# Moving squares between two phases of an attention and MLP kernel, splitting masks, and reordering value matmuls

## The chip, the cores and the metric

One core of a Trainium2 chip runs the whole program. The metric is the device time of one execution in microseconds (us). Several executions are timed; a kernel that is compared with the kernel before runs in alternating rounds with it on the same chip. Ratios are computed as the mean time of one kernel's fast runs over that of the other's of the same rounds, so they are not quite the ratio of the medians that are quoted.

## The reference, cut to what matters

```python
# q, k, v: 8 batches, 8 heads, 576 positions, head size 64; s: 8 x 8 x 576
scores = scale * q @ k.T + minimum(-(cum_i - cum_j), 0)     # causal, cum = cumsum(relu(s))
attn   = softmax(scores); x = attn @ v                       # 4608 tokens x 512
out    = gelu(x @ w_in) @ w_out                              # 512 -> 2048 -> 512
```

## The kernel before, the parts that matter

The MLP runs over nine chunks of 512 tokens. In chunk c it does the first layer (`l1_item`, eight items of eight matmuls, each with a gelu on ScalarE), then the second layer (`l2_item`, 16 groups). Beside the second layer stands the attention of the next batch b = c + 1: scores, exponentials, masks, value matmuls. Between the exponentials and the gelus the kernel loads ScalarE's table of functions anew, 16 times in all: `exp_set` and `gelu_set` are the loads, 1.28 us each in the trace.

```python
def square_v(b, st):                       # only the sum is used; sq is written and never read
    sq = work.tile([128, S * 2], bf16, tag="sq", bufs=1, name="sq")
    nc.scalar.activation(sq[:n_st, : H * D], raws[b, "v"][...], func=AF.Square,
                         accum_out=sumv[:n_st, b, st : st + 1])

def l1_item(c, f2, n0=0, n1=NB):
    h_ps = ps.tile([128, 2, NB], fp32, tag="sc", bufs=2, name="h_ps")     # ... cut
    ...                                     # 8 matmuls into h_ps
    nc.scalar.activation(gT_of[c][:, f2*2 : f2*2+2, n0:n1], h_ps, func=AF.Gelu)

# second layer of chunk c, side work of batch b = c + 1 (chunks 1 to 6):
sc_at = (2, 5, 7, 9) if b < 4 else (2, 5, 8, 11)     # groups at which scores stand
...
for st in range(ST):
    side[sc_at[3]].append((square_v, b, st))          # after the last exponentials
side[sc_at[3]].append((gelu_set,))                    # then the table for the next first layer
```

The squares feed a check that the fast formula is safe; they are needed at the end only.

Of the kernel before, what the change touches and what calls it, by code (L numbers as in the profile page):

```python
# [19 lines left out]
def kernel(  # L20
# [21 lines left out]
    ST = 5  # L42
# [151 lines left out]

    def square_qk(g, i):

        sq = work.tile([128, S * 2], bf16, tag="sq", bufs=1, name="sq")
        nc.scalar.activation(
            sq, raws[0, "qk"][:, i, g, :], func=AF.Square, scale=D ** -0.5,
            accum_out=ssq[:, g, i : i + 1],  # L200
        )

# [5 lines left out]

    def square_v(b, st):
        n_st = 128 if st < ST - 1 else SL  # L210
        sq = work.tile([128, S * 2], bf16, tag="sq", bufs=1, name="sq")
        nc.scalar.activation(  # L212
            sq[:n_st, : H * D], raws[b, "v"][:n_st, st].rearrange("p h d -> p (h d)"), func=AF.Square,
            accum_out=sumv[:n_st, b, st : st + 1],
        )

# [142 lines left out]
                P[:, 2 * h2 : 2 * h2 + 2, o : o + 512], s_ps[h2], func=AF.Exp, scale=scale  # L359
            )  # L360

    def mk_item(b, g, u):
        P = P_of[b, g]
        o = UO[u]
        d = P[:, :, o : o + 512].rearrange("p e (g c) -> p e g c", c=256)[:, :, :, 0:128]
        nc.vector.tensor_tensor(  # L366
            d, d, tri_bf.unsqueeze(1).unsqueeze(1).to_broadcast([128, 4, 2, 128]), op=MULT
        )
        if u == 1:
            d = P[:, :, o + 448 : o + 512]  # L370
            nc.vector.tensor_tensor(
                d, d, tri_bf[:, :64].unsqueeze(1).to_broadcast([128, 4, 64]), op=MULT
            )
# [40 lines left out]
    def filler(n, lhsT=None):  # L414

        f_ps = yps.tile([128, NB], fp32, tag="mlp", bufs=2, name="f_ps")
        for _ in range(n):
            nc.tensor.matmul(  # L418
                f_ps, lhsT=zero[:, :128] if lhsT is None else lhsT, rhs=zero, start=True, stop=True
            )  # L420
# [7 lines left out]
    def av_item(b, g, it, later=False):  # L428
        P = P_of[b, g]
        n = 128 if it < ST - 1 else SL  # L430
        o_ps = ps.tile([128, 4, D + 1], fp32, tag="av", bufs=2, name="av")
        for h in range(4):
            for i, (jt, off) in enumerate(BLK[it]):
                nc.tensor.matmul(  # L434
                    o_ps[:, h, :],
                    lhsT=P[:, h, off : off + 128],
                    rhs=vv[b % 2][:, jt, 4 * g + h, :],
                    start=(i == 0), stop=(i == len(BLK[it]) - 1),
                )
        if g == 0:  # L440
            x_of[b, it] = work.tile([128, H * D], bf16, tag="x", bufs=6, name="x")
        rc = work.tile([128, 4], fp32, tag="rc", bufs=3, name="rc")
        nc.vector.reciprocal(rc[:n], o_ps[:n, :, D])  # L443
        nc.vector.tensor_tensor(  # L444
            x_of[b, it][:n, g * 256 : g * 256 + 256].rearrange("p (h d) -> p h d", d=D),
            o_ps[:n, :, 0:D],
            rc[:n].unsqueeze(2).to_broadcast([n, 4, D]),
            op=MULT,
        )
        if g == HG - 1 and b > 0 and not later:  # L450
            to_xT(b, it)
# [92 lines left out]
    sc_first(1, 0, (1,))  # L544
    av_item(0, 0, 0)
    filler(1)
    av_item(0, 0, 1)
    sc_first(0, 1, (1,))
    mk_item(0, 1, 0)
    sc_first(1, 1, (0,))  # L550
    av_item(0, 1, 0)
    av_item(0, 1, 1)
    sc_first(1, 1, (1,), 0)
    to_xT(0, 0, True)
    filler(2)
    to_xT(0, 1, True)
    filler(2)
    mk_item(0, 0, 1)
    scale_v(0, 2)
    mk_item(0, 1, 1)  # L560
# [9 lines left out]
    for c in range(NCH):  # L570
        b = c + 1
        if c > 0 and b + 1 < B:
            load_qks(b + 1)
            load_v(b + 1, nc.gpsimd)
        if c == 0:

            late = [
                [], [], [], [(av, 0, 0, 2), (av, 0, 1, 2)], [(av, 0, 0, 3)],
                [(av, 0, 1, 3), (to_xT, 0, 2, True)], [(to_xT, 0, 3, True)],
                [(scale_v, 0, 4), (av, 0, 0, 4)],  # L580
                [(av, 0, 1, 4), (to_xT, 0, 4, True)],
            ] + [[]] * 7
            for half in range(2):
                for f2 in range(FT // 2):
                    l1_item(0, f2, half * 256, half * 256 + 256)
                    for f, *a in late[8 * half + f2]:
                        f(*a)
                    if f2 % 2 and 3 <= 8 * half + f2 <= 11:
                        square_v(0, 4 * half + f2 // 2 - 1)
        else:  # L590
            for f2 in range(FT // 2):
                l1_item(c, f2)
                for g, it in late_of.get(c, [])[f2 : f2 + 1]:
                    av(c, g, it)
                if b < B and f2 < HG:
                    tr_qk(b, 0, f2)
                    tr_qk(b, 1, f2)
                if b < B and f2 == 2:
                    den_col(b)
                    for st in range(2):  # L600
                        scale_v(b, st)
                if b < B and f2 == 3:
                    for st in range(2, ST):
                        scale_v(b, st)
                if b < B and 4 <= f2 < 4 + HG:
                    absmax(b, f2 - 4)
                if c == 2 and f2 == 7:
                    cert_decay()
                if c == 1 and 1 <= f2 <= ST:
                    square_v(c, f2 - 1)  # L610
        if b < B:
            if c == 0:
                for g in range(HG):
                    for i in range(2):
                        tr_qk(b, i, g)
                den_col(b)
            exp_set()
            if c == 0:
                load_qks(2)
                load_v(2, nc.gpsimd)  # L620
                side = [[] for _ in range(16)]
                side[0] = [(sc, b, 0, 0), (scale_v, b, 0), (scale_v, b, 1), (mk, b, 0, 0)]
                side[3] = [(sc, b, 1, 0), (mk, b, 1, 0)]
                side[5] = [(sc, b, 0, 1), (av, b, 0, 0), (av, b, 0, 1)]
                side[6] = [(scale_v, b, 2), (av, b, 1, 0, True), (mk, b, 0, 1)]
                side[7] = [(sc, b, 1, 1), (av, b, 1, 1, True), (to_xT, b, 0, True)]
                side[8] = [(scale_v, b, 3), (av, b, 0, 2), (to_xT, b, 1, True), (gelu_set,), (mk, b, 1, 1)]
                side[9] = [(av, b, 0, 3)]
                side[11] = [(av, b, 1, 2, True), (scale_v, b, 4), (square_qk, 0, 0), (square_qk, 0, 1)]
                side[12] = [(av, b, 1, 3, True), (square_qk, 1, 0), (square_qk, 1, 1)]  # L630
                side[13] = [(to_xT, b, 2, True)]
                side[14] = [(to_xT, b, 3, True)]
                groups(c, (0, 1), side[:8])
                for sub in (2, 3):
                    groups(c, (sub,), side[4 * sub : 4 * sub + 4])
            else:

                side = [[] for _ in range(16)]
                sc_at = (2, 5, 7, 9) if b < 4 else (2, 5, 8, 11)
                for at, (g, u) in zip(sc_at, [(0, 0), (1, 0), (0, 1), (1, 1)]):  # L640
                    side[at].append((sc, b, g, u))
                for st in range(ST):
                    side[sc_at[3]].append((square_v, b, st))
                side[sc_at[3]].append((gelu_set,))
                for at, (g, u) in zip((5, 8, 10 if b < 4 else 11, 12 if b < 4 else 14), [(0, 0), (1, 0), (0, 1), (1, 1)]):
                    side[at].append((mk, b, g, u))
                for at, (g, it) in zip((6, 7, 9, 10), [(0, 0), (0, 1), (1, 0), (1, 1)]):
                    side[at].append((av, b, g, it))
                if b < 4:
                    side[12].append((av, b, 0, 2))  # L650
                    side[13].append((av, b, 1, 2, True))
                    side[14].append((to_xT, b, 2, True))
                if c == 1:
                    side[0].extend([(absmax, c, 0), (absmax, c, 1)])
                    side[3].append((cert_exp,))
                for sub in range(4):
                    groups(c, (sub,), side[4 * sub : 4 * sub + 4])
        else:
            for sub in range(4):
                l2_item(c, (sub,), store=(c, sub) < LAST)  # L660
                if c == B - 1:
                    (cert_1, cert_2, cert_3, cert_4)[sub]()
# [172 lines left out]
```

## Time and profile before

| | before |
|---|---|
| median of three runs | 318.3 us (318.27 to 318.76) |
| span of the profiled run | 316.6 us, granted clock 1.000 |
| TensorE / ScalarE / VectorE busy | 96% / 61% / 63% |
| chunk 0's first layer, its second layer, chunk 1's first layer begin | 18.93, 36.22, 56.60 us |
| from chunk 1's first layer to the last second layer (the "body") | 241.11 us |

Below, PE is TensorE, ACT ScalarE, DVE VectorE. A line of a timeline gives start, length, engine, source line, operation, output<-input, shapes, count, and in brackets the idle time before with what ended it. A line of the table of waits gives waiter, what was waited for, total us, number and longest. Shown ends of matmuls are modelled: one of the second layer is shown with 379 ns and the next starts after 216, so a true wait is about 0.16 us longer than the shown one.

### The profile page before, as it was taken

Reading aid. Unit: us, or ns where it says so; the run is one execution under the profiler, and the core shown is the slowest. Engines: PE = TensorE matmul, PEld = TensorE weight load, DVE = VectorE, ACT = ScalarE, POOL = GpSimd, SP = SyncE. Lnnn points to the kernel's source line nnn. Section 1 sums busy time; section 2 is a strip of 40 time slices with the busy share of each in tenths; the row PEclk is TensorE's granted clock in tenths of the full one; section 3 lists DMA queues with packets and bytes.
Section 4 is the critical chain, followed back from the end, with each engine's and each line's share of the span. In section 5 each row is a group of like instructions: output and inputs, shape, how many; then the busy total and the mean of one; then the engine's idle time right before and its main releaser. Section 6 shows DMA issues by size and latency. Waiting matters only on the chain. (4 is left out here: it accounts for less than half of the span.)

```text
span 316.6 us, 6078 instructions
## 1 busy us (share of the span) xinstructions
PE 303.5 (96%) x2480; PEld 156.1 (49%) x2523; DVE 199.9 (63%) x400; ACT 192.9 (61%) x256; POOL 52.9 (17%) x72
## 2 busy tenths in 40 slices
PE   8999998999999999999999999999999999999993
PEld 3587754444554455445444444444444545444441
DVE  7876658699769766965697559945894632250020
ACT  2786976887765687564956676657756685105500
POOL 8543440125070006000240004000000000000000
PEclk9999999999999999999999999999999999999999
DMA  7999999669869215932399158412110321010012
GB/s 133 220 230 209 226 212 277 129 111 211 187 176 185 64 53 155 196 59 76 97 176 162 66 101 160 35 56 79 52 24 34 101 51 25 33 69 33 1 69 75
DMA packets 30980, 36.48 MB, mean 115 GB/s; under 512 B 15648, under 2 KB 20000, under 8 KB 30944
## 3 DMA queue, kind: packets, MB, share of 16 engines
q0 software_dynamic: 11552, 23.07, 38.5%
q1 hardware_dynamic: 19248, 12.80, 15.7%
q8 instruction: 22, 0.36, 0.5%
q14 instruction: 14, 0.11, 0.2%
q10 hardware_dynamic: 144, 0.13, 0.1%
HBM read 36.85 MB, written 9.44 MB: 146 GB/s over the span
## 5 line engine op out<-in xcount | busy, mean ns | idle before, releaser
L466 PE MATMUL h_ps<-xT,w_in_r 128*128 128x512 bf16 (+1 forms) x626 | 131.7, 357 | 2.8 <-ACT gT L471 2.0
L482 PE MATMUL o_ps<-w_out_r,gT 128*128 128x512 bf16 x549 | 132.3, 379 | 2.2 <-issue 1.3
L471 ACT ACTIVATE gT<-h_ps 128x1024 bf16<-128x1024 f32 (+1 forms) x80 | 74.6, 938 | 63.7 <-PE h_ps L466 62.9
L466 PEld LDWEIGHTS <-w_in_r 128*128 128x128 bf16 x640 | 60.0, 98 | 56.5 <-issue 2.9
L482 PEld LDWEIGHTS <-gT 128*128 128x128 bf16 x576 | 52.0, 98 | 56.5 <-issue 3.1
L358 ACT ACTIVATE P<-sc_ps 128x1024 bf16<-128x1024 f32 x56 | 54.3, 1021 | 30.7 <-PE sc_ps L343 30.7
L122 POOL DMA_DIRECT2D raw_v<-in_v_dram x40 | 34.0, 864 | 119.7 <-ACT sq L212 107.4
L492 DVE COPY o_sb<-o_ps 128x512 f32<-128x512 f32 x32 | 22.1, 691 | 48.5 <-PE o_ps L482 48.5
L443 DVE RECIPROCAL rc<-av 128x4 f32<-128x4 f32 (+1 forms) x80 | 14.0, 175 | 40.2 <-PE av L434 40.2
L187 DVE STREAM_TRANSPOSE qkT<-raw_qk 128x576 f32<-128x576 f32 x32 | 37.4, 1242 | 0.9 <-DMA raw_qk<-in_k_dram 0.6
L434 PEld LDWEIGHTS <-P 128*128 128x128 bf16 x576 | 27.2, 98 | 17.4 <-DVE x L444 1.6
L444 DVE TENSOR_TENSOR x<-av,rc 128x256 bf16<-128x256 f32 (+1 forms) x80 | 33.8, 423 | 3.0
L204 DVE TENSOR_REDUCE amx<-raw_qk 128x2 f32<-128x2304 bf16 x14 | 35.1, 2535 | 0.0
L434 PE MATMUL av<-vv,P 128*128 128x65 bf16 x576 | 30.4, 193 | 1.0 <-DVE x L444 0.7
L220 DVE TENSOR_TENSOR vv<-raw_v,wb 128x512 bf16<-128x512 f32 (+1 forms) x40 | 26.0, 689 | 3.2 <-DMA raw_v<-in_v_dram 3.2
L366 DVE TENSOR_TENSOR P<-P,tri_bf 128x1024 bf16<-128x1024 bf16 x32 | 21.9, 684 | 8.8 <-ACT P L358 8.8
L212 ACT ACTIVATE sq<-raw_v 128x512 bf16<-128x512 f32 (+1 forms) x40 | 25.1, 628 | 0.8
L343 PE MATMUL sc_ps<-qkT 32*128 32x256 bf16 (+2 forms) x560 | 18.2, 250 | 0.1
L343 PEld LDWEIGHTS <-qkT 32*128 32x128 bf16 x560 | 11.7, 92 | 12.7 <-issue 12.0
L418 PE MATMUL f_ps<-zero 128*128 128x512 bf16 x32 | 11.2, 468 | 1.3 <-DVE zero L150 1.2
L497 ACT ACT_TABLE_LOAD x8 | 10.3, 1283 | 0.9 <-PEq L819 0.7
L500 ACT ACT_TABLE_LOAD x8 | 10.3, 1283 | 0.1
(79 smaller groups left out, 90.2 us busy)
## 6 DMA issues: line engine op xcount, KB each, us to landing
out_dram<-o_sb SPq DMA_DIRECT2D x35, 256.0 KB, 2.2
raw_v<-in_v_dram POOLq DMA_DIRECT2D x32, 256.0 KB, 6.3
raw_qk<-in_q_dram POOLq DMA_DIRECT2D x7, 576.0 KB, 9.0
raw_qk<-in_k_dram POOLq DMA_DIRECT2D x7, 576.0 KB, 11.9
w_in_r<-in_moe_w_in_dram POOLq DMA_DIRECT2D x4, 512.0 KB, 12.0
w_out_r<-in_moe_w_out_dram POOLq DMA_DIRECT2D x4, 512.0 KB, 16.4
raw_v<-in_v_dram POOLq DMA_DIRECT2D x8, 128.0 KB, 8.0
raw_qk<-in_q_dram POOLq DMA_DIRECT2D x2, 288.0 KB, 5.6
```

The costliest lines, as they stand in the source:

```text
L122: eng.dma_start(out=t[:n_st, st, :, :], in_=bass.AP(tensor=v.tensor, offset=v.offset + b * H * S * D + st * 128 * D, ap=[[D, n_st], [S * D ...
L187: nc.vector.transpose(qkT[b % 2][:, i, g, :S, :].rearrange("p s e -> p (s e)").bitcast(fp32) .rearrange("p (l j) -> p j l", j=LT), raws[b, ...
L204: nc.vector.tensor_reduce(amx[:, b * HG + g], raws[b, "qk"][:, :, g, :], axis=AX, op=ALU.max, apply_absolute_value=True,)
L212: nc.scalar.activation(sq[:n_st, : H * D], raws[b, "v"][:n_st, st].rearrange("p h d -> p (h d)"), func=AF.Square, accum_out=sumv[:n_st, b, ...
L220: nc.vector.tensor_tensor(vv[b % 2][:n_st, st, :, 0:D], raws[b, "v"][:n_st, st, :, :], w.unsqueeze(2).to_broadcast([n_st, H, D]), op=MULT,)
L343: nc.tensor.matmul(s_ps[h // 2][:, h % 2, off : off + n], lhsT=qk[r, 1, g, jt * 128 : jt * 128 + 128, e], rhs=qk[r, 0, g, i0 : i0 + n, e], ...
L358: nc.scalar.activation(P[:, 2 * h2 : 2 * h2 + 2, o : o + 512], s_ps[h2], func=AF.Exp, scale=scale)
L434: nc.tensor.matmul(o_ps[:, h, :], lhsT=P[:, h, off : off + 128], rhs=vv[b % 2][:, jt, 4 * g + h, :], start=(i == 0), stop=(i == len(BLK[it ...
L444: nc.vector.tensor_tensor(x_of[b, it][:n, g * 256 : g * 256 + 256].rearrange("p (h d) -> p h d", d=D), o_ps[:n, :, 0:D], rc[:n].unsqueeze( ...
L466: nc.tensor.matmul(h_ps[:, i, :], lhsT=w_in_r[:, ko, ft * 128 : (ft + 1) * 128], rhs=xT[:, ko, c * NB + n0 : c * NB + n1], start=(ko == 0) ...
L471: nc.scalar.activation(gT_of[c][:, f2 * 2 : f2 * 2 + 2, n0:n1], h_ps, func=AF.Gelu)
L482: nc.tensor.matmul(y_of[c, sub], lhsT=gT[:, ft, sub * 128 : (sub + 1) * 128], rhs=w_out_r[:, ft, :], start=(ft == 0), stop=(ft == FT - 1),)
```

## The change

The intent: take the squares of v away from the stretch between the last exponentials and the next gelus, and tighten the start of the kernel and chunk 0's second layer. Cut to its core:

```diff
 def square_qk(g, i):                         # batch 0
-    sq = work.tile([128, S * 2], bf16, tag="sq", bufs=1, name="sq")
-    nc.scalar.activation(sq, raws[0, "qk"][:, i, g, :], ...)
+    r = raws[0, "qk"][:, i, g, :]
+    nc.scalar.activation(r, r, ...)
 def square_v(b, st):
-    sq = work.tile([128, S * 2], bf16, tag="sq", bufs=1, name="sq")
+    sq = work.tile([128, H * D], bf16, tag="sq", bufs=2, name="sq")
 ... mk_item takes h0, h1: a part of the heads
 # start
+    mk_item(0, 1, 0, 0, 2)
     av_item(0, 0, 1)
+    mk_item(0, 1, 0, 2, 4)
     sc_first(0, 1, (1,))
-    mk_item(0, 1, 0)
-    sc_first(1, 1, (0,))
+    filler(1)
     av_item(0, 1, 0)
     av_item(0, 1, 1)
+    sc_first(1, 1, (0,), 0)
+    to_xT(0, 0, True)
+    filler(1)
+    to_xT(0, 1, True)
     sc_first(1, 1, (1,), 0)
-    to_xT(0, 0, True)
-    filler(2)
-    to_xT(0, 1, True)
-    filler(2)
 # first layer, chunks 1 to 7
-                if c == 1 and 1 <= f2 <= ST:
-                    square_v(c, f2 - 1)
+                if f2 < ST and c < B:
+                    square_v(c, f2)
 # chunk 0's second layer
-                side[6] = [(scale_v, b, 2), (av, b, 1, 0, True), (mk, b, 0, 1)]
-                side[7] = [(sc, b, 1, 1), (av, b, 1, 1, True), (to_xT, b, 0, True)]
-                side[8] = [(scale_v, b, 3), (av, b, 0, 2), (to_xT, b, 1, True), ...]
+                side[6] = [(av, b, 1, 0, True), (av, b, 1, 1, True), (scale_v, b, 2), (mk, b, 0, 1)]
+                side[7] = [(to_xT, b, 0, True), (sc, b, 1, 1)]
+                side[8] = [(to_xT, b, 1, True), (scale_v, b, 3), (av, b, 0, 2), ...]
 # later second layers
-                for st in range(ST):
-                    side[sc_at[3]].append((square_v, b, st))
                 side[sc_at[3]].append((gelu_set,))
```

More of the change, by code (lines that the diff above doesn't have):

```diff
@@ L195, in square_qk @@
     def square_qk(g, i):
-        sq = work.tile([128, S * 2], bf16, tag="sq", bufs=1, name="sq")
+        r = raws[0, "qk"][:, i, g, :]
         nc.scalar.activation(
-            sq, raws[0, "qk"][:, i, g, :], func=AF.Square, scale=D ** -0.5,
+            r, r, func=AF.Square, scale=D ** -0.5,
             accum_out=ssq[:, g, i : i + 1],
@@ L210, in square_v @@
         n_st = 128 if st < ST - 1 else SL
-        sq = work.tile([128, S * 2], bf16, tag="sq", bufs=1, name="sq")
+        sq = work.tile([128, H * D], bf16, tag="sq", bufs=2, name="sq")
         nc.scalar.activation(
-            sq[:n_st, : H * D], raws[b, "v"][:n_st, st].rearrange("p h d -> p (h d)"), func=AF.Square,
+            sq[:n_st], raws[b, "v"][:n_st, st].rearrange("p h d -> p (h d)"), func=AF.Square,
             accum_out=sumv[:n_st, b, st : st + 1],
@@ L360, in sc_item, with mk_item @@
             )
-    def mk_item(b, g, u):
+    def mk_item(b, g, u, h0=0, h1=4):
         P = P_of[b, g]
         o = UO[u]
-        d = P[:, :, o : o + 512].rearrange("p e (g c) -> p e g c", c=256)[:, :, :, 0:128]
+        d = P[:, h0:h1, o : o + 512].rearrange("p e (g c) -> p e g c", c=256)[:, :, :, 0:128]
         nc.vector.tensor_tensor(
-            d, d, tri_bf.unsqueeze(1).unsqueeze(1).to_broadcast([128, 4, 2, 128]), op=MULT
+            d, d, tri_bf.unsqueeze(1).unsqueeze(1).to_broadcast([128, h1 - h0, 2, 128]), op=MULT
         )
@@ L624 @@
                 side[5] = [(sc, b, 0, 1), (av, b, 0, 0), (av, b, 0, 1)]
-                side[6] = [(scale_v, b, 2), (av, b, 1, 0, True), (mk, b, 0, 1)]
-                side[7] = [(sc, b, 1, 1), (av, b, 1, 1, True), (to_xT, b, 0, True)]
-                side[8] = [(scale_v, b, 3), (av, b, 0, 2), (to_xT, b, 1, True), (gelu_set,), (mk, b, 1, 1)]
+                side[6] = [(av, b, 1, 0, True), (av, b, 1, 1, True), (scale_v, b, 2), (mk, b, 0, 1)]
+                side[7] = [(to_xT, b, 0, True), (sc, b, 1, 1)]
+                side[8] = [(to_xT, b, 1, True), (scale_v, b, 3), (av, b, 0, 2), (gelu_set,), (mk, b, 1, 1)]
                 side[9] = [(av, b, 0, 3)]
```

## The prediction

> **What bounds the kernel now.** I began with the page's table of busy time and its groups of instructions (columns: line, engine, operation, output<-inputs, count | busy us, mean ns of one | idle us before, by releaser).
>
> ```profile
> PE 303.5 (96%) x2480; PEld 156.1 (49%) x2523; DVE 199.9 (63%) x400; ACT 192.9 (61%) x256; POOL 52.9 (17%) x72
> ...
> L466 PE MATMUL h_ps<-xT,w_in_r 128*128 128x512 bf16 (+1 forms) x626 | 131.7, 357 | 2.8 <-ACT gT L471 2.0
> L482 PE MATMUL o_ps<-w_out_r,gT 128*128 128x512 bf16 x549 | 132.3, 379 | 2.2 <-issue 1.3
> ```
>
> TensorE (PE) is the bound and is nearly full, so only its gaps can be won. Part of the idle time is not real: L482 should have 576 records and shows 549, and a missing one of 0.22 us leaves a gap put down to "issue" (8 gaps, 0.2 us the longest). The table of waits, longest in total first (total us, number, longest), names the true ones inside the body:
>
> ```profile
> PE h_ps L466 <- ACT gT L471: 2.0, 4, 0.5
> ...
> PE av L434 <- DVE x L444: 0.7, 1, 0.7
> ...
> PE xt_ps L409 <- DVE x L444: 0.6, 1, 0.6
> ```
>
> The first line is four equal waits, so something repeats. The timeline of PE finds it in each of the four steps whose first layers begin at 154.03, 187.19, 220 and 254 us. It never occurs in the two steps before them. Here is one (start, length, engine, line, what, count [idle before]):
>
> ```profile
> 157.72 0.41 PE L434 MATMUL av<-vv,P 128*128 128x65 bf16 x8
> 158.62 1.89 PE L466 MATMUL h_ps<-xT,w_in_r 128*128 128x512 bf16 x7 [0.50 <-ACT gT L471]
> ```
>
> The eight value matmuls take 0.24 us in other places (160.34 to 160.59), so L466 was due at 157.96 and began at 158.62. The true loss is 0.66 us, not 0.50, because the shown end of a matmul lies about 0.16 us after the next one could start (379 ns shown, 216 ns pitch). ScalarE (ACT) in the same stretch:
>
> ```profile
> 150.67 1.94 ACT L358 ACTIVATE P<-sc_ps 128x1024 bf16<-128x1024 f32 x2 [1.70 <-PE sc_ps L343]
> 152.50 0.63 ACT L212 ACTIVATE sq<-raw_v 128x512 bf16<-128x512 f32 x1
> 153.01 0.20 ACT L212 ACTIVATION_READ_ACCUMULATOR sq<-raw_v 128x1 f32 x1
> ...
> 156.25 1.28 ACT L500 ACT_TABLE_LOAD   x1
> 157.55 1.94 ACT L471 ACTIVATE gT<-h_ps 128x1024 bf16<-128x1024 f32 x2
> ```
>
> Five squares of v stand between the last exponentials and the table load: 152.50 to 156.25. The first h_ps was full about 155.75, but its gelu starts at 157.55. h_ps has two buffers, so the third l1 item waits for that gelu to end at 158.57. In the two earlier steps the last scores lie two groups sooner and gelu is ready in time (table load 121.42 to 122.70, first gelu 123.93, waiting for PE).
>
> **What the Trainium skill says.** "ScalarE: Activation LUTs", What ACT_TABLE_LOAD costs: about 1283 ns for the load and about 1380 ns for a drain; 186 ns + 0.833 ns per element for an ACTIVATE with immediate operands. The trace agrees on the load (x8, mean 1283 ns) and on the square (613 ns for 512 elements against 628), but shows no drain: the load ends at 157.53 and gelu starts at 157.55. "TensorE: Matmul & The Clock Gate", section "Wait — 56ns, not 53.3ns?": 215.7 ns start to start for 512 columns at full clock; here 16 matmuls of the first layer take 3.46 us, 216 each, and the granted clock is 1.00. "Perfetto Trace Analysis", Identifying the Most-Contended Engine: matmul busy share is a poor measure of room left. The trace agrees: the ends overlap the next starts. Same page, Summary of the profiler window per engine type: the window of a DMA issued by GpSimd ends with descriptor generation, not with the data. I therefore read landing times; w_in's last piece is issued at 11.15 for 0.75 us and lands 14.1 us after its issue.
>
> **The change, part by part.**
>
> Squares of v into the next first layer. The same 35 squares remain, but 5 x 0.75 us (0.63 plus the 0.19 accumulator read, pitch 153.25 - 152.50) leave the path before the table load. In the four slow steps the load runs from 152.5 to 153.8, 1.9 us before the first h_ps is full. The wait vanishes: 4 x 0.66 = 2.6 us. Inside the first layer ACT then has gelu 0.94 + square 0.75 = 1.69 us per item. PE needs 8 x 0.216 = 1.73 us per item, 1.97 with a value item, and two h_ps buffers absorb the rest. The step at 58 us already runs so without a wait of PE: gelus at 62.46, 64.19, 65.91, 67.64, each with a square between, 1.73 apart. In the two earlier steps nothing is won, since nothing was lost. The v buffer now comes free after the fifth l1 item, some 7 us later (about 163.5 instead of 156.5 in the step shown). Issue takes 4.2 us and landing 6.3, so it is there by 175; scale_v needs it in the next first layer, after 187. Hidden.
>
> Squares of batch 0's q, k in place. Four instructions of 1162 ns before and after, same place, same types. 0.
>
> Masks by halves, fewer fillers, at the start. Three fillers of 0.216 us go (the order of instructions shows six PE rows fewer). The mask of 684 ns becomes two of about 0.42. The chain is set by DVE, though. From its timeline: x of group 0's first item ends at 14.95, the half mask at 15.3, the second x at 15.8, the second half mask at 16.2; then the value matmuls end at 16.5 (16.70 now). Two pairs of reciprocal and x take 1.1 us, and two transposes and copies follow. Working the list through, the first layer starts at 18.65 instead of 18.93: 0.3 us. But the first pass over l1 meets w_in's last piece: it lands at 25.25, and the item that uses it begins on PE at 25.36 with no idle before. An earlier arrival turns into a wait there, so I count 0.05.
>
> Value matmuls of group 1 moved up, chunk 0's second layer. The wait to remove is at 48.75 (0.69 shown, 0.85 true: the four l2 matmuls from 47.04 end at 47.90):
>
> ```profile
> 47.04 1.03 PE L482 MATMUL o_ps<-w_out_r,gT 128*128 128x512 bf16 x4
> 48.75 0.42 PE L434 MATMUL av<-vv,P 128*128 128x65 bf16 x8 [0.69 <-DVE x L444]
> ```
>
> It waits for a PSUM buffer that DVE must read, and DVE is busy without a gap from 45.50 to 49.0. In the new order the buffer that this item waits for is the copy of the first transpose. DVE must do before it, from 45.2: two pairs (1.1), scale_v (0.61), the masks (0.60 + 0.20), the o_sb copy (0.60), the copy itself (0.42). That ends at about 48.75 as well. The second value item gets a new wait of 0.2 near 45.0 for its buffer. What is gained is that the second transpose (0.22 us) is already done. I count 0.2.
>
> Sum: 2.6 + 0.05 + 0.2 = 2.85; 318.3 - 2.85 = 315.4.
>
> **The rivals.** (a) ACT becomes late in the first layer: 1.69 of 1.73 us is tight. Against it is the step at 58 us, which does it; if it failed, seven steps with five squares would lose perhaps 0.1 each, and the time would be 316. (b) The later v loads collide with transposing DMAs of x, which must land before the next first layer (the one at 150.09 is needed at 154). The DMA share after 168 us is moderate (page: slices of 20 to 90%), and the loads should be over first. If not, up to six steps wait 0.3 us: 317. (c) The startup gain is not eaten by w_in: 0.3 more, and the second layer's DVE chain loosens: 0.4 more, 314.7. For it: three fillers do go. Against: landings of 25.25 (w_in), 40.8 and 43.6 (w_out), against uses at 25.36, 41.01 and 44.04. (d) The four waits only shift to another engine. DVE runs without a gap through those first layers (156.75 to 172), but its value items end 2 us before PE needs their buffers, so 0.66 fits.
>
> **Range and chances.** The four waits are sure in place and size; I give them 2.3 to 2.7. The two early parts together may give -0.3 to +1.0. With 0.3 us of spread between runs that is 314.5 to 316.3. A gain over 2% needs 6.4 us; all named waits of PE in the body sum to less than 5, so 2 in 100. A loss over 2% would need a new wait of a microsecond in every step: 1 in 100.
>
> **What would show it right or wrong.** The line "h_ps <- gT" leaves PE's waits, and a step of the four shortens from 33.16 us (table loads at 171.19 and 204.35) to 32.5. In those steps the first gelu waits for PE. Squares stand between gelus, with no PE wait. The first layer starts near 18.65, and a wait or a gap for w_in shows near 25.3. In chunk 0 a wait of value matmuls for DVE remains, about 0.3 to 0.5 shown near 48.5. The prediction is wrong if steps do not shorten, if a new wait of h_ps or xT repeats by step, or if the first second layer starts over 0.4 us earlier than 36.22.

## The result, and the profile after

The changed kernel took 315.73 us in the median of four runs (315.04 to 316.02) against 318.53 (318.27 to 319.59); the ratio of fast runs is 0.9903, with a 95% interval of 0.9874 to 0.9931. That is inside the predicted range; the predicted point was 315.4. The interval leaves out 1, so a gain of about 1% is clear of the noise.

The first lines are the busy times and the group of the first layer's matmuls on the changed kernel's page, and then its whole table of PE waits without those put down to "issue":

```profile
PE 301.7 (96%) x2478; PEld 155.6 (50%) x2520; DVE 200.0 (64%) x401; ACT 190.0 (61%) x256; POOL 53.0 (17%) x72
...
L467 PE MATMUL h_ps<-xT,w_in_r 128*128 128x512 bf16 (+1 forms) x625 | 131.4, 357 | 0.8
```

```profile
PE f_ps L419 <- DVE zero L150: 1.2, 1, 1.2
PE xt_ps L410 <- DVE x L445: 0.6, 1, 0.6
PE sc_ps L389 <- DVE qkT L187: 0.4, 1, 0.4
PE av L435 <- DVE P L367: 0.3, 1, 0.3
PE av L435 <- DVE xT L413: 0.3, 1, 0.3
PE av L435 <- DVE vv L221: 0.2, 1, 0.2
PE t_ps L244 <- ACT cum L238: 0.2, 1, 0.2
```

The line "h_ps <- ACT gT" with its four waits is gone, and the first layer's idle time before it falls from 2.8 to 0.8 us. In the timelines of PE and ACT the step that the prediction took as its example now looks so:

```profile
156.97 0.41 PE L435 MATMUL av<-vv,P 128*128 128x65 bf16 x8
157.22 1.89 PE L467 MATMUL h_ps<-xT,w_in_r 128*128 128x512 bf16 x7
```

```profile
149.92 1.94 ACT L359 ACTIVATE P<-sc_ps 128x1024 bf16<-128x1024 f32 x2 [1.70 <-PE sc_ps L344]
151.88 1.28 ACT L501 ACT_TABLE_LOAD   x1
155.26 1.02 ACT L472 ACTIVATE gT<-h_ps 128x1024 bf16<-128x1024 f32 x1 [2.10 <-PE h_ps L467]
156.19 0.62 ACT L213 ACTIVATE sq<-raw_v 128x512 bf16<-128x512 f32 x1
156.71 0.19 ACT L213 ACTIVATION_READ_ACCUMULATOR sq<-raw_v 128x1 f32 x1
157.17 1.02 ACT L472 ACTIVATE gT<-h_ps 128x1024 bf16<-128x1024 f32 x1 [0.28 <-PE h_ps L467]
```

The third item follows the value matmuls at once. The table is loaded right after the exponentials, and gelu waits 2.10 us for PE instead of the reverse. Every gelu of this first layer still waits a little for PE, so the squares between them delay nothing.

Where the 3.35 us of span went can be read from four positions. Chunk 1's first layer begins at 55.85 instead of 56.60, so the front gave 0.75. The body takes 238.63 instead of 241.11, so it gave 2.48. The stretch after it is 0.12 shorter, which no run explains. The front's 0.75 splits into 0.14 before any changed instruction (the first filler matmuls took 5.46 us instead of 6.14, and waits of 0.19 and 0.35 us for `cum` and `qkT` took most of that back), 0.27 in the start and 0.34 in chunk 0's second layer.

### The profile page after: what moved, and what is told of

It is laid out like the page before. It is cut to its first block, busy times and chain, and to the rows that moved or that the text cites. A ratio compares the mean times of both kernels' runs of the same rounds, so it can differ in the third digit from the quotient of the medians.

```text
span 313.3 us, 6063 instructions
## 1 busy us (share of the span) xinstructions
PE 301.7 (96%) x2478; PEld 155.6 (50%) x2520; DVE 200.0 (64%) x401; ACT 190.0 (61%) x256; POOL 53.0 (17%) x72
## 5 line engine op out<-in xcount | busy, mean ns | idle before, releaser
L367 DVE TENSOR_TENSOR P<-P,tri_bf 128x1024 bf16<-128x1024 bf16 (+1 forms) x33 | 22.1, 669 | 8.7 <-ACT P L359 8.7
L213 ACT ACTIVATE sq<-raw_v 128x512 bf16<-128x512 f32 (+1 forms) x40 | 24.9, 622 | 0.0
L419 PE MATMUL f_ps<-zero 128*128 128x512 bf16 x29 | 9.4, 448 | 1.2 <-DVE zero L150 1.2
```

The lines of the kernel that those rows point to most:

```text
L213: nc.scalar.activation(sq[:n_st], raws[b, "v"][:n_st, st].rearrange("p h d -> p (h d)"), func=AF.Square, accum_out=sumv[:n_st, b, st : st ...
```

## The experiments

Times are medians; "front" is when chunk 1's first layer begins, "body" the time from there to the start of the last second layer, both from the profiled run. One run of e4_three_more (339.56 us) and one of e9_inplace_only (325.34 us) were slow: the medians hold them, the ratios do not. The run profiled for e6_av_up_only was the slowest of its eight (319.87 us).

| run | us, this / before | ratio (95% interval) | front | body |
|---|---|---|---|---|
| before | | | 56.60 | 241.11 |
| the change | 315.73 / 318.53 | 0.9903 (0.9874 to 0.9931) | 55.85 | 238.63 |
| e1_sqv_only | 316.18 / 318.71 | 0.9912 (0.9889 to 0.9934) | 56.67 | 238.61 |
| e2_sqv_back | 316.16 / 318.71 | 0.9925 (0.9902 to 0.9948) | 55.97 | 238.98 |
| e3_one_of_five | 316.39 / 318.71 | 0.9926 (0.9904 to 0.9948) | 56.30 | 238.52 |
| e4_three_more | 333.28 / 318.71 | 1.0445 (1.0407 to 1.0484) | 56.62 | 253.73 |
| e5_start_only | 318.34 / 318.38 | 1.0000 (0.9979 to 1.0021) | 56.35 | 241.13 |
| e6_av_up_only | 318.37 / 318.38 | 0.9994 (0.9978 to 1.0010) | 57.13 | 241.12 |
| e7_no_mask | 316.17 / 318.38 | 0.9937 (0.9908 to 0.9966) | 56.69 | 238.51 |
| e9_inplace_only | 319.07 / 318.38 | 1.0022 (0.9997 to 1.0047) | 56.67 | 241.12 |
| e12_two_buffers | 316.49 / 318.60 | 0.9926 (0.9911 to 0.9941) | 56.57 | 238.81 |
| after_again | 316.14 / 318.60 | 0.9917 (0.9902 to 0.9932) | 56.46 | 238.50 |
| e10_late | 314.86 / 318.60 | 0.9879 (0.9863 to 0.9896) | 55.30 | 238.51 |
| e11_late_av | 315.04 / 318.60 | 0.9880 (0.9863 to 0.9897) | 55.38 | 238.52 |

The bodies of kernels without a change to the squares of v agree within 0.02 us. The fronts scatter, and the reason comes below. A variant with a third buffer for raw v, meant to test the later loads, did not fit into the memory and was not run.

### The squares of v moved alone

```diff
-                if c == 1 and 1 <= f2 <= ST:
-                    square_v(c, f2 - 1)
+                if f2 < ST and c < B:
+                    square_v(c, f2)
-                for st in range(ST):
-                    side[sc_at[3]].append((square_v, b, st))
```

> The kernel before with only the 35 squares of v moved into the next first layer. My theory (the five squares hold back the table load in four steps, 0.66 us of PE each): -2.6 us, 315.9 against 318.5; the wait of h_ps for gT leaves PE's waits; the four steps shorten from 33.16 to 32.5 us. Rival A (squares between the gelus make ACT late, 0.1 in seven steps): only -1.9. Rival B (most of the measured gain comes from the start and chunk 0): -1 or less.

The body fell by 2.50 us, the four waits left the table, and the ratio is 0.9912. The table loads that open two neighbouring second layers stand 32.51 us apart (138.10 and 170.61), before 33.17. This part alone gives what the prediction said. The squares between the gelus cost little: the body is within 0.1 us of that of the run below in which only one square stands there.

### The change without the moved squares

```diff
-                if f2 < ST and c < B:
-                    square_v(c, f2)
+                if c == 1 and 1 <= f2 <= ST:
+                    square_v(c, f2 - 1)
+                for st in range(ST):
+                    side[sc_at[3]].append((square_v, b, st))
```

> The changed kernel with the squares of v put back where they were. My theory: it keeps only what start and chunk 0 gave, 0.28 + 0.34 = 0.6 us (318.5 to 317.9), with the four waits of 0.66 us back. Prediction on record gave these parts 0.25. If parts interact: clearly more or less than 0.6.

This is a miss. With all five squares back ahead of the table load, 2.13 of the body's 2.48 us stayed. The timelines of ACT and PE of this run show why:

```profile
151.89 0.63 ACT L213 ACTIVATE sq<-raw_v 128x512 bf16<-128x512 f32 x1
152.41 0.20 ACT L213 ACTIVATION_READ_ACCUMULATOR sq<-raw_v 128x1 f32 x1
152.50 0.63 ACT L213 ACTIVATE sq<-raw_v 128x512 bf16<-128x512 f32 x1
...
155.07 1.28 ACT L501 ACT_TABLE_LOAD   x1
156.36 1.98 ACT L472 ACTIVATE gT<-h_ps 128x1024 bf16<-128x1024 f32 x2
```

```profile
157.12 0.41 PE L435 MATMUL av<-vv,P 128*128 128x65 bf16 x8
157.44 1.89 PE L467 MATMUL h_ps<-xT,w_in_r 128*128 128x512 bf16 x8
```

A square follows the one before after 0.61 us, where the kernel before needed 0.75. The five squares and the way to the load take 3.18 us instead of 3.75 (before: 152.50 to 156.25). PE resumes at 157.44, when 157.12 + 0.24 = 157.36 was due: a wait of 0.08 instead of 0.66. The one difference that bears on the pitch is the line of the diff that gives `sq` two buffers. (The same line makes the tile narrower, 512 columns instead of 1152. No run separates the two for v, but the squares of q and k below keep their width and gain 0.12 us each by no longer sharing the tile.) Nobody reads `sq`. But with one buffer each square starts only after the accumulator read of the square before has ended: in the kernel before that read runs from 153.01 to 153.22 and the next square starts at 153.25. With two buffers the square at 152.50 starts before the read that ends at 152.61. My working had passed over that line.

### Only one of the five squares moved

```diff
+                if f2 == 0 and 1 < c < B:
+                    square_v(c, ST - 1)
-                for st in range(ST):
+                for st in range(ST - 1):
                     side[sc_at[3]].append((square_v, b, st))
```

> The kernel before, four of five squares left in place, only the fifth moved behind the first gelu of the next first layer. My theory is a threshold: 0.75 us less ahead of the table load ends gelu at 157.8 in the step shown, 0.16 before the third item is due at 157.96, so the whole 2.6 us are won. Rival (gain in proportion to the squares moved): a fifth, 0.5 us.

The body fell by 2.59 us, so one square of five wins all. In the timelines of ACT and PE the table load begins at 155.21, the first gelu ends at 157.53, and the third item follows the value matmuls at once:

```profile
155.21 1.28 ACT L500 ACT_TABLE_LOAD   x1
156.51 1.02 ACT L471 ACTIVATE gT<-h_ps 128x1024 bf16<-128x1024 f32 x1
```

```profile
157.44 0.41 PE L434 MATMUL av<-vv,P 128*128 128x65 bf16 x8
157.68 1.89 PE L466 MATMUL h_ps<-xT,w_in_r 128*128 128x512 bf16 x8
```

The gain is a threshold and not a share of the moved work. That also explains why the moved squares and the second buffer, 2.5 and 2.1 to 2.3 us alone, do not add: each takes away 0.57 us or more of a wait of 0.66.

### Three squares more

```diff
-                for st in range(ST):
+                for st in [0, 1, 2, 0, 1, 2, 3, 4]:
                     side[sc_at[3]].append((square_v, b, st))
```

> The kernel before, eight squares instead of five before the table load (three done twice, result unchanged). My theory: past the threshold each square costs PE its full 0.75 us: 3 x 0.75 = 2.25 more per step in the four steps, +9.0 us; the steps of c=1 and c=2 have about 2.2 us of room and lose 0 to 0.1. So about +9 us, 327.5, and four waits of about 2.9 us. Rival (ACT has other room, PE not held): under +4.

The waits are as expected: 11.0 us shown in four, the longest 2.8. But the body grew by 12.62 us, not by 9. The table loads that open the second layers are 35.44, 37.09 and 37.10 us apart. The first figure is the 33.17 of before plus 2.27, which is three squares. The other two have 1.65 more. The table of windows shows a lower clock in one of these two steps, and the timeline of PE slower matmuls in both (busy times of PE, weight loads, DVE, ACT, POOL, then the granted clock as the mean of the window, DMA share and GB/s):

```profile
196.00:200.00 4.00, 3.44 (x17) 1.61 (x17) 1.48 (x2) 1.79 (x3) 2.68 (x4) 0.64 1.04 209
```

```profile
161.13 1.89 PE L466 MATMUL h_ps<-xT,w_in_r 128*128 128x512 bf16 x8 [2.76 <-ACT gT L471]
...
196.56 3.03 PE L466 MATMUL h_ps<-xT,w_in_r 128*128 128x512 bf16 x8 [2.75 <-ACT gT L471]
233.66 2.59 PE L466 MATMUL h_ps<-xT,w_in_r 128*128 128x512 bf16 x8 [2.76 <-ACT gT L471]
```

After two of the four waits the granted clock fell: eight matmuls took 3.03 and 2.59 us instead of 1.89. Shorter windows show it at 0.50 from 197.2 to 200.5 and from 234.75 to 238.05, and at 1.00 before and after. These two steps lose 2 x 1.65 = 3.3 us more; with 9.0 for the waits and 0.2 in the steps of c = 1 and 2 the sum is 12.5 of 12.62. So the linear part of the model held, and a wait of almost 3 us has a second price that the 0.66 us wait did not have.

Why two of the four and not all can be guessed from the trace's record of the clock. The two falls start at 197.14 and 234.69 us and last 3.41 us each; their distance, 37.55 us, is 11.0 times that length. If the clock is judged in consecutive stretches of 3.41 us, the waits that a fall followed made PE idle for 2.8 and 2.4 us of the stretch at whose end the fall begins, and the other two waits for at most 1.5 and 1.9 of any one. This rests on one trace and was not tested. The runs of this kernel scatter more than the others, from 330.92 to 334.51 us in the fast state.

### The start alone, chunk 0's order alone, the mask left out

The start alone, its main lines (`mk_item` with parts of the heads as in the change):

```diff
+    mk_item(0, 1, 0, 0, 2)
     av_item(0, 0, 1)
+    mk_item(0, 1, 0, 2, 4)
     sc_first(0, 1, (1,))
-    mk_item(0, 1, 0)
-    sc_first(1, 1, (0,))
+    filler(1)
 ...                                   # the rest of the start as in the change
```

> The kernel before with only the start changed (masks by halves, order, three fillers fewer). On record: the first layer starts 0.3 us sooner, but the item that uses w_in's last piece waits for its landing, so 0.05 is left. What the trace of the changed kernel suggests: 0.28 us passes through unchanged to the first second layer (first layer's first pass of the same length, 17.29 us), total -0.28.

From the second score block of group 1 (13.23 us) to the first layer (18.69) this run takes 5.46 us; the kernel before takes 5.73 (13.20 to 18.93). The start is worth 0.27 us, as worked out. It went through to the second layer at 35.97 us (36.22 before). The prediction had it stopped by the landing of w_in's last piece. That landing, however, came at about 11.16 + 13.8 = 24.96 in this run and at about 25.25 in the kernel before: it moved along by itself, which is luck. The timed ratio, 1.0000, cannot show so little.

Chunk 0's order alone:

```diff
-                side[6] = [(scale_v, b, 2), (av, b, 1, 0, True), (mk, b, 0, 1)]
+                side[6] = [(av, b, 1, 0, True), (av, b, 1, 1, True), (scale_v, b, 2), (mk, b, 0, 1)]
 ...                                   # side[7] and side[8] as in the change
```

> The kernel before with only chunk 0's second layer reordered (group 1's value matmuls moved up). On record -0.2: the wait for DVE stays, only the transpose is done inside it. From the trace of the changed kernel: second layer 20.04 instead of 20.38 us, -0.34. If the wait had been removed whole: -0.85.

Here the second layer took 20.39 us (36.74 to 57.13), no gain, for a reason that the expectation did not have. The timeline of PE has a wait for a weight:

```profile
42.13 1.89 PE L482 MATMUL o_ps<-w_out_r,gT 128*128 128x512 bf16 x8 [0.53 <-DMA w_out_r<-in_moe_w_out_dram]
```

The piece of w_out was issued at 26.11 and landed 16.0 later, at 42.11. Of this wait (0.69 with the modelled end) about half comes on top. Three runs with this order have such a wait: 0.69 us here, 0.49 in the repeat of the change, 0.74 in the first version of the last section. Their second layers are 0.35, 0.13 and 0.38 us longer than the 20.04 of the changed kernel. So 0.34 to 0.36 us of the wait is absorbed each time, and by this reckoning the order alone would have taken about 20.04 here, as expected.

The mask left out, on the changed kernel:

```diff
-    mk_item(0, 1, 0, 0, 2)
-    mk_item(0, 1, 0, 2, 4)
```

> The changed kernel without the start's two half masks (0.76 us of DVE less; result wrong on purpose). The first layer would then start 0.5 to 0.7 us sooner. If w_in's landing is a wall (on record): the seventh item of the first pass starts no sooner than the landing near 25, a gap shows before it, and at most 0.1 us of the gain arrives at the second layer. If it is not: that item starts 0.5 us before 24.95 and the second layer begins 0.5 us before 35.81.

Its output is wrong, which doesn't matter for the time. The stretch that took 5.46 us took 4.95, so 0.51 was won there. But in this run the inputs landed late (PE waited 0.7 us for k), and w_in's last piece landed at 12.23 + 13.5 = 25.73, just ahead of its use at 25.78. It does not decide the question of the wall. The run with the squares put back does: there the first layer began at 18.09, 0.43 sooner than in the changed kernel. Its item with w_in's last piece still began at 25.05, right at the landing (10.44 + 14.6 = 25.04), and its second layer began at 35.93, later than the 35.81 of the changed kernel. The table of waits for 17 to 27 us of that run names it, at the weight loads:

```profile
PEld L467 <- DMA w_in_r<-in_moe_w_in_dram: 0.5, 2, 0.3
```

### The squares of q and k in place, alone

```diff
-        sq = work.tile([128, S * 2], bf16, tag="sq", bufs=1, name="sq")
-        nc.scalar.activation(sq, raws[0, "qk"][:, i, g, :], ...)
+        r = raws[0, "qk"][:, i, g, :]
+        nc.scalar.activation(r, r, ...)
```

> The kernel before with only batch 0's squares of q, k done in place. Both on record and now: 0 within 0.1 us; the pitch of these squares falls from 1.27 to 1.15 us (as in the changed kernel's trace), which no wait of PE rests on.

The body is 241.12 us: nothing, as said. The pitch of these four squares fell from 1.27 to 1.15 us, because they too no longer share one `sq`. The squares of v kept theirs, at 0.755.

### The second buffer alone

```diff
 # the in-place squares as above, and
-        sq = work.tile([128, S * 2], bf16, tag="sq", bufs=1, name="sq")
+        sq = work.tile([128, H * D], bf16, tag="sq", bufs=2, name="sq")
 ...                                   # the call writes sq[:n_st], as in the change
```

> The kernel before, squares of v where they were, but with a second buffer for the tile they write and nobody reads (q, k squares in place to make room, which the run before showed to be worth 0). Theory from the run with the squares put back: the single buffer makes each square wait for the write of the one before, pitch 0.755 us; with two it is 0.61, five squares end 0.57 us sooner, and the wait of PE falls from 0.66 to 0.09 in four steps: chunk 1's first layer to the last second layer 238.98 us instead of 241.11, -2.1. Rival (the gain of that run came from the start's part): 241.1, 0.

The body is 238.81 us, 2.30 less, and the table of PE's waits has no line for h_ps and gT any more. In the timelines of ACT and PE a square follows after 0.61 us, and PE's third item begins at 158.02, where 157.69 + 0.24 = 157.93 was due: 0.09 is left.

```profile
152.47 0.63 ACT L213 ACTIVATE sq<-raw_v 128x512 bf16<-128x512 f32 x1
152.99 0.20 ACT L213 ACTIVATION_READ_ACCUMULATOR sq<-raw_v 128x1 f32 x1
153.08 0.63 ACT L213 ACTIVATE sq<-raw_v 128x512 bf16<-128x512 f32 x1
```

```profile
157.69 0.41 PE L435 MATMUL av<-vv,P 128*128 128x65 bf16 x8
158.02 1.89 PE L467 MATMUL h_ps<-xT,w_in_r 128*128 128x512 bf16 x7
```

So one buffer more, with no instruction moved, gives nine tenths of the gain in the body.

### Two versions that go further

The first takes two waits out of the first pass of chunk 0, the second also moves two value items one group later.

```diff
-                [(av, 0, 1, 3), (to_xT, 0, 2, True)], [(to_xT, 0, 3, True)],
-                [(scale_v, 0, 4), (av, 0, 0, 4)],
-                [(av, 0, 1, 4), (to_xT, 0, 4, True)],
+                [(av, 0, 1, 3), (to_xT, 0, 2, True)], [(scale_v, 0, 4), (to_xT, 0, 3, True)],
+                [(av, 0, 0, 4)],
+                [(av, 0, 1, 4)], [(to_xT, 0, 4, True)],
 # and in the second version, for chunk 0's second layer
-                side[8] = [(to_xT, b, 1, True), (scale_v, b, 3), (av, b, 0, 2), ...]
-                side[9] = [(av, b, 0, 3)]
+                side[8] = [(to_xT, b, 1, True), (scale_v, b, 3), ...]
+                side[9] = [(av, b, 0, 2)]
+                side[10] = [(av, b, 0, 3)]
```

The changed kernel ran again beside them:

> The changed kernel once more, beside the others of this job. -2.5 us in the body (238.63), front 55.8 to 56.5 as the landings of the weights fall; 0.990 to 0.992 of the time before.

> The changed kernel with two waits of the first pass over l1 taken out (scale_v of the fifth block before a copy, the last transpose one item later): 0.36 + 0.72 = 1.07 us of PE. If only PE's own order bounds the front: second layer 1.07 us sooner, -1.0 against the changed kernel. If the landings of the weights are the wall (w_in near 25, w_out's third piece near 41 and its last near 43): the gain is met by a wait for w_out, and 0.3 or less is left.

> As the one before, and chunk 0's value items of block 2 and 3 one group later, which takes out the wait of 0.46 us (0.30 shown) for the copy of the transpose. -0.4 against the one before, if nothing that lands later than 44 us holds it: chunk 0's second layer 19.6 instead of 20.04 us apart from any wait for w_out.

The repeat gave 0.9917 and a body of 238.50. The two versions gave 0.9879 and 0.9880, about 1.2 us below the repeat by the medians (314.86 and 315.04 against 316.14); their intervals lie below the repeat's. How much of that the edits earn is not settled: in the profiled runs the first layer began at 18.09 and 18.43 us against 19.00 in the repeat, before any line that they touch. The edited first pass took 16.79 and 16.66 us instead of 17.29, so 0.50 and 0.63 of the expected 1.07 arrived at the second layer; the table of waits has 0.5 us for w_in in each. So part of the gain met the wall, as the second theory had it. In the first version the second layer begins at 34.88 us, and then the group that first uses w_out's third piece waits:

```profile
40.31 1.89 PE L483 MATMUL o_ps<-w_out_r,gT 128*128 128x512 bf16 x7 [0.58 <-DMA w_out_r<-in_moe_w_out_dram]
```

That is 0.74 us with the modelled end, 0.38 of it on top (20.42 us for the layer). In the second version the wait is 0.90 shown, since the piece came at 40.84 in that run. From there to chunk 1's first layer it takes 14.54 us where the first version takes 14.99: the reordering is worth its 0.45, and the later landing took most of it away again (20.29 us).

## Why the prediction was right or wrong, point by point

**The four waits.** Right in place, cause and size. The squares moved alone gave 2.50 us, worked out as 2.6. In the change 2.48 to 2.61 were won. In one of the later steps of the changed kernel a first layer starts 0.12 us late (185.91). The repeat of the kernel does not show this, and the run with only chunk 0's order changed, in which no square moved, has a like delay of 0.10 (187.84). What holds it was not settled.

**"The same 35 squares remain", pitch 0.75.** This step was incomplete. The diff also gave `sq` a second buffer, which brings the pitch to 0.61. Alone it gives 2.30 us. The time came out right because the two parts remove the same wait.

**Squares of q, k in place.** Right: 0 in the body. The pitch changed, off the path.

**The start, "I count 0.05".** The working to 0.3 was right (0.27 measured). The step that let w_in's landing eat it was right as a mechanism: the table of waits has weight loads held by w_in in four runs (0.5 us with the squares put back, 0.2 with three squares more, 0.5 in each of the last two versions). It was wrong as a fixed wall: the landing fell between about 24.8 and 25.8 us in the runs, so the gain passes in some and not in others. In the profiled run of the changed kernel it passed by luck: the piece landed at about 24.9 and was used at 24.95, and 0.27 arrived, not 0.05. By the prediction's own sign ("wrong if … the first second layer starts over 0.4 us earlier than 36.22") this step failed there, though barely: that layer started at 35.81, 0.41 earlier, of which 0.14 was there before any changed line. In the repeat it started at 36.29.

**Chunk 0's second layer, "I count 0.2".** The step that fell short is the cause of the wait at 48.75. I read it as DVE having too much to do, which is half of it. In the seven profiled runs with the old order that item starts 3.24 to 3.25 us after the scaling of v's third block, always. That is DVE's work, and with v in time it leaves a shown wait of 0.28. But the scaling itself waits for its data in the kernel before, but not in the run with only the squares moved (the first fence is the kernel before, the second the other run; the item starts at 48.75 and 48.83):

```profile
45.50 0.70 DVE L220 TENSOR_TENSOR vv<-raw_v,wb 128x512 bf16<-128x512 f32 x1 [0.31 <-DMA raw_v<-in_v_dram]
```

```profile
45.59 0.68 DVE L220 TENSOR_TENSOR vv<-raw_v,wb 128x512 bf16<-128x512 f32 x1
```

In the second run the layer had begun 0.48 us later (36.70), and it took 19.97 us in the old order. The seven runs of the old order fit this: where the scaling starts as soon as DVE is free, the layer takes 19.96 or 19.97 us (three runs), where it starts 0.10 later 20.08 or 20.10 (two), and where it starts 0.40 later 20.38 (two). The new order takes 20.04 in the runs without a wait for w_out. The reordering wins 0.34 us against a load as late as that of the kernel before, and loses 0.07 against one in time. In the profiled run of the changed kernel v's third block landed about 8.8 us after the layer began (9.2 in the kernel before, 8.7 in the second run above). By this reckoning the old order would have taken about 20.0 there too: that 0.34 is the luck of the load. The prediction's step had no term for it. What the prediction had right is when the item starts, 12.59 us into the layer against 12.53 before. The new wait that the prediction named, for the copy of the transpose, is there (0.30 shown).

**The rivals.** (a) Late squares between gelus: no, every gelu of the step shown waits for PE. (b) Later v loads against the transposes: the tables show no wait of that kind. (c) A start that w_in does not eat and a looser second layer in chunk 0: in the changed kernel's profiled run both came, 0.27 and 0.34, with the landings as their reason. (d) The wait moving to another engine: no.

**The sum.** 2.6 + 0.05 + 0.2 came to 2.85 against 2.8 by the medians. The body gave 2.5 of it; the rest, here 0.27 + 0.34, depends on when loads land. That the sum fits so well is partly luck: the two early parts were taken at 0.25 and gave 0.61 in the profiled run, and single runs of the changed kernel scatter by 1 us (315.04 to 316.02) where the range allowed 0.3.

## What to carry to other kernels

A wait behind a chain of small operations acted as a threshold here: find how much must leave the chain (here 0.66 us per step), and the cheapest way to take that much away is enough. A tile that is only written still tied its writers together when it had one buffer (0.755 us apart, 0.61 with two), so look at the pitch of a run of equal instructions and not only at their length. Where loads saturate the start of a kernel, read landings against uses before counting a gain there, and expect it to differ from run to run.

## What the Trainium skill lacked or had wrong

- "ScalarE: Activation LUTs", What ACT_TABLE_LOAD costs: gives a drain of about 1380 ns with every switch. No run shows it: in the changed kernel the exponentials end at 151.86, the load stands at 151.88 for 1.28 us; in the kernel before gelu starts 0.02 us after the load.
- "ScalarE: Activation LUTs", What it computes: names an accumulator output without its price. Here it is a second instruction of 0.19 us, and a square of 512 elements with it has a pitch of 0.61 us.
- "ScalarE: Activation LUTs", same section as the first point: says that back-to-back ACTIVATEs overlap by about 93 ns. It does not say what writing the same tile costs: a square with its accumulator read follows the one before after 0.755 us when they share one buffer and after 0.61 with two.
- "TensorE: Matmul & The Clock Gate", HAM oscillation: gives "no PE-idle gaps >~3.4µs" as the rule. The table at the end of the page, under "Why this matters for your kernels", has ~3 µs instead. Here the granted clock fell after two of four gaps of 2.75 and 2.76 us (2.9 with the modelled end), to 0.50 for 3.4 us, which cost 1.65 us each.
